# Other PSUM banks for the transposed blocks and the inverse transform's blocks in two stretches of a hand-ordered FFT and mixture-of-experts kernel

## The chip, the cores and the metric

The kernel runs on one core of a Trainium2 chip. The metric is the device time of one execution in microseconds (us). Three runs of the kernel before are known, and one profiled execution.

## What is computed

A filter in the frequency domain, then a layer of eight experts of which each token uses two:

```python
X = np.fft.rfft(x, axis=1)                       # x: 8 batches, 2496 tokens, 256 channels
y = np.fft.irfft(X * (filt_r + 1j * filt_i), n=2496, axis=1)
x = y.reshape(19968, 256)
noisy = x @ w_gate + np.log1p(np.exp(x @ w_noise)) * noise
top2 = np.argpartition(-noisy, 2, axis=1)[:, :2]     # two experts of eight
w = softmax over the two chosen values
for e in range(8):
    out[mask] += w * (np.maximum(x[mask] @ w1[e], 0) @ w2[e])   # 256 -> 1024 -> 256
```

## The kernel before

The transform of length 2496 is split as 39 x 64. One batch is two halves n of 128 channels each, so batch 0 is n = 0 and 1, batch 1 is n = 2 and 3. Each half goes through a chain of steps on TensorE, and each step writes one PSUM tile of 128 x 512 that ScalarE or VectorE copies out:

- `s1` (L320): the transform over 39, tile `q1` (in a few places `u3`); `kg1` (L401): the transform over 64, tile `q3`, then the product with the filter on VectorE (L424, L425); `kg2` (L434): the inverse over 64, tile `q4`, copied to `G` (L448).
- `logit_half` (L450), `logits` (L471), `gating` (L488): the gate's logits, tiles `u1`, `u2` and `lg`. From `lg` the generator `gate` (L744) works out the two experts of every token. This is a long row of small VectorE operations, with two exponentials and a logarithm on ScalarE (L757, L760, L790). Three times TensorE helps it with tiny matmuls: `rk` (L812 to L814) needs `rs` (L796); `sl` (L883, L884) needs `new` (L878); `st` (L908) needs `sval` (L904).
- `t3` (L506): four 128 x 120 blocks of `G` are transposed into tile `q5`, and ScalarE copies it to `tf` (L517). `i2` (L526): one matmul per `tf` into tile `q6`, the inverse over 39, which ScalarE copies to `yt` (L546) and a DMA writes to memory (L553). Each half has six such pairs.
- `route` (L918) turns the choice into a list of rows per expert, with tile `ra` (L950). Then the experts' blocks of up to 512 rows run: `turn` (L1061) makes the transposed rows, `expert` (L1149) multiplies with w1 in three passes (L123 to L125) into `hps` tiles, applies ReLU (L1181, L1182), and multiplies with w2 into `yps` tiles. Weights are split into two parts on ScalarE and VectorE (L1137, L1138).

TensorE runs the experts' first products between the last `t3` and `i2` of batch 1.

What sets the order. Batches 0 and 1 run "early", by a plan that is written out by hand: `plan` (L596 to L649) gives each of some 32 slots a list of steps. `pin` (L166) ties what each step issues on an engine behind what the step before it issued there. The gate's steps are traced at a place of the plan but are not tied; a scheduler places them when the program is built. For batch 1 the plan's slot 26 holds `logit_half`, `logits`, `gating`, then the first three `t3` and two `i2` and two `s1`; at that slot's end all of `rk`, `sl` and `st` are traced (L667 to L674). Slots 27 to 31 hold the other `t3`, `i2` and `s1`. Within an engine, the order is fixed once the program is built.

What sets the banks. PSUM has eight banks, given out under four tags. `ps` (L299) looks up the tag of a tile's name; names that are not in the table get `fps`. Tiles of one tag take its banks in turn, and a tile whose bank is still being read has to wait.

```python
EARLY = {"q1": "hps", "q2": "hps", "q5": "yps", "q6": "yps", "u1": "xps", "u3": "hps"}
BANKS = {"hps": 2, "yps": 2, "xps": 1, "fps": 3}
tag = self.banks.get(nm, "fps") if self.early else "fps"
return self.PS.tile([128, 512], F32, tag=tag, name=nm, bufs=BANKS[tag])
```

So `u2`, `lg`, `rk`, `sl`, `st` and `ra` always use the three `fps` banks. `MOVES` changes the table at the start of a slot: at slot 12, at slot 14 (where `t3` and `i2` of batch 0 share `hps`) and at slot 26 (where those of batch 1 share `yps`).

Of the kernel before, what the change touches and what calls it, by code (L numbers as in the profile page):

```python
# [137 lines left out]
EARLY = {"q1": "hps", "q2": "hps", "q5": "yps", "q6": "yps", "u1": "xps", "u3": "hps"}  # L138
BANKS = {"hps": 2, "yps": 2, "xps": 1, "fps": 3}

MOVES = {0: {"q3": "yps"}, 12: {"q3": "fps"}, 14: {"q3": "yps", "q4": "yps", "q5": "hps", "q6": "hps"}, 26: {"q1": "xps", "q4": "fps", "q5": "yps", "q6": "yps"}}


class Moe:
# [412 lines left out]
    def fft_stream(self):  # L557
# [105 lines left out]
        for t in range(max(plan) + 1):  # L663
            self.banks.update(MOVES.get(t, {}))
            for g in plan.get(t, []):
# [669 lines left out]
```

## Time and profile before

| what | value |
|---|---|
| median of three runs | 2246.81 us |
| lowest and highest run | 2244.74 and 2250.58 us |
| the profiled execution's own time | 2249.04 us |
| span of its profile | 2247.3 us |
| mean clock that TensorE was granted | 0.997 |
| TensorE matmuls busy | 2202.3 us (98%) |
| VectorE busy | 1614.5 us (72%) |
| ScalarE busy | 1227.9 us (55%) |
| GpSimd busy | 945.7 us (42%) |

A row of the timeline reads: start, duration, engine, line, operation, output<-input, shape, count, and in brackets the idle time before it with what ended it. Times in it are counted from the span's start. A row of the windows reads: the stretch, its length, then busy time of TensorE matmuls (PE), its weight loads (PEld), VectorE (DVE), ScalarE (ACT) and GpSimd (POOL) with counts, TensorE's granted clock, the DMA share and GB/s. A row of the waits reads: who waited for whom, the total in us, how often, and the longest.

### The profile page before, as it was taken

What the parts mean: (1) busy time and instruction counts of PE and PEld (TensorE: products, weight loads), DVE (VectorE), ACT (ScalarE), POOL (GpSimd) and SP (SyncE); (2) the same over time, 40 slices, a digit from 0 to 9 for tenths busy, and PEclk for the clock granted to TensorE, in tenths of its full rate; (3) what the DMA queues carried; (4) which work ended last, traced back from release to release, by engine and by line L of the source; (5) the groups of instructions that cost most, each with busy time, mean ns of one, the idle gap of its engine ahead of it and who ended that gap; (6) DMA issues with size and microseconds to landing.
All of it is one profiled execution on the core that took longest, in us unless ns stands there. A gap on an engine that the chain in (4) does not pass through costs nothing.

```text
span 2247.3 us, 39485 instructions
## 1 busy us (share of the span) xinstructions
PE 2202.3 (98%) x12687; PEld 1847.3 (82%) x12687; DVE 1614.5 (72%) x3482; ACT 1227.9 (55%) x2415; POOL 945.7 (42%) x824
## 2 busy tenths in 40 slices
PE   8999999999999999999999999999999999999998
PEld 6658888888888888888888888878888888888887
DVE  4777778779877968797668857796555556667776
ACT  6475655665565456545554445544444344557776
POOL 4014335334433543444434534444545454544442
PEclk9999999999999999999999999999999999999999
DMA  8768778987887677666665657556555557787774
GB/s 246 229 198 221 190 174 182 211 212 166 196 195 180 150 167 170 142 158 155 145 153 125 147 116 174 111 124 122 110 125 114 126 109 156 154 209 201 208 197 127
DMA packets 435434, 370.57 MB, mean 165 GB/s; under 512 B 185643, under 2 KB 345363, under 8 KB 435219
## 3 DMA queue, kind: packets, MB, share of 16 engines
q1 hardware_dynamic: 373907, 283.58, 46.7%
q0 software_dynamic: 61312, 84.40, 23.4%
q8 instruction: 101, 1.65, 0.3%
q14 instruction: 114, 0.93, 0.1%
HBM read 227.73 MB, written 105.25 MB: 148 GB/s over the span
## 4 chain that ended last, share of the span: by engine, by line
PE 89%; DVE 3%; DMA 3%; ACT 2%; issue 2%; SPq 0%; POOL 0%; another core or an unknown queue 0%; POOLq 0%; DVEq 0%; ACTq 0%
PE yps L1210 20%; PE hps L123 13%; PE hps L125 13%; PE hps L124 12%; PE yps L1211 10%; PE q L446 3%; PE yps L125 3%; PE yps L123 3%; PE yps L124 3%; PE q L512 1%; DMA stage<-w 1%; PE u L459 1%; PE q L536 1%; PE q L329 1%; PE q L534 1%
## 5 line engine op out<-in xcount | busy, mean ns | idle before, releaser
L1218 POOL DMA_INDIRECT out<-stage,ids x316 | 535.7, 1695 | 415.8 <-DVE stage L1217 224.4
L1210 PE MATMUL yps<-w,hh 128*128 128x512 f32 x1952 | 690.2, 398 | 4.0 <-DVE stage L1217 2.6
L1027 POOL DMA_INDIRECT stage<-y,ids x316 | 328.5, 1040 | 582.8 <-DMA xt<-stage 424.6
L124 PE MATMUL hps<-mxl,w1h 128*128 128x512 f32 (+2 forms) x1424 | 529.7, 374 | 1.5 <-DVE mxl L1091 1.5
L123 PE MATMUL hps<-mxh,w1h 128*128 128x512 f32 (+2 forms) x1424 | 518.9, 377 | 5.2 <-DVE hl L1182 3.7
L125 PE MATMUL hps<-mxh,w1l 128*128 128x512 f32 (+2 forms) x1424 | 523.9, 370 | 0.0
L1211 PE MATMUL yps<-w,hl 128*128 128x256 f32 x1952 | 521.7, 281 | 0.0
L1182 DVE SCALAR_TENSOR_TENSOR hl<-hps,hh 128x512 fp32r<-128x512 f32 (+2 forms) x712 | 433.5, 624 | 97.4 <-ACT hh L1181 88.1
L1181 ACT ACTIVATE hh<-hps 128x512 fp32r<-128x512 f32 (+2 forms) x712 | 381.5, 555 | 183.4 <-PE hps L125 163.6
L1210 PEld LDWEIGHTS yps<-w,hh 128*128 128x128 f32 x1952 | 356.7, 188 | 82.2 <-issue 5.3
L1211 PEld LDWEIGHTS yps<-w,hl 128*128 128x128 f32 x1952 | 367.1, 188 | 26.3 <-issue 0.6
L1215 ACT ACTIVATE stage<-yps,gt 128x256 f32<-128x256 f32 x316 | 142.3, 478 | 348.9 <-PE yps L1211 177.8
L125 PEld LDWEIGHTS hps<-mxh,w1l 128*128 128x128 f32 x1424 | 268.0, 188 | 48.1
L123 PEld LDWEIGHTS hps<-mxh,w1h 128*128 128x128 f32 x1424 | 263.4, 188 | 50.5 <-DVE hl L1182 9.1
L124 PEld LDWEIGHTS hps<-mxl,w1h 128*128 128x128 f32 x1424 | 268.1, 188 | 42.8 <-DVE mxl L1091 2.0
L1217 DVE SCALAR_TENSOR_TENSOR stage<-yps,gt,stage 128x256 f32<-128x256 f32 x244 | 112.1, 479 | 215.7 <-ACT stage L1215 185.3
L1137 ACT CAST w1h<-stage 128x512 fp32r<-128x512 f32 x192 | 119.2, 622 | 113.2 <-DMA stage<-w 52.9
L1138 DVE TENSOR_TENSOR w1l<-stage,w1h 128x512 fp32r<-128x512 f32 x192 | 130.8, 686 | 56.7 <-ACT w1h L1137 46.6
L123 PE MATMUL yps<-w,hh 128*128 128x256 f32 x576 | 163.4, 288 | 4.0 <-ACT hh L1181 3.0
L125 PE MATMUL yps<-w,hl 128*128 128x256 f32 x576 | 159.2, 285 | 1.1 <-DVE hl L1182 1.1
L124 PE MATMUL yps<-w,hh 128*128 128x256 f32 x576 | 160.1, 284 | 0.0
L1138 DVE TENSOR_TENSOR w<-stage,w 128x512 fp32r<-128x512 f32 x228 | 152.7, 685 | 6.7 <-ACT w L1137 5.3
(231 smaller groups left out, 3044.4 us busy)
## 6 DMA issues: line engine op xcount, KB each, us to landing
stage<-w SPq DMA_DIRECT2D x420, 256.0 KB
x<-x SPq DMA_DIRECT2D x88, 256.0 KB
wb<-w SPq DMA_DIRECT2D x18, 1024.0 KB
fx<-fd SPq DMA_DIRECT2D x140, 128.0 KB
fd<-c SPq DMA_DIRECT2D x73, 240.0 KB
out<-z SPq DMA_DIRECT2D x24, 702.0 KB
y<-yt SPq DMA_DIRECT2D x40, 248.6 KB
y<-yt SPq DMA_DIRECT2D x40, 234.0 KB
```

The lines of the kernel that those rows point to most:

```text
L123: nc.tensor.matmul(o, lh, rh, start=start, stop=False)
L124: nc.tensor.matmul(o, lh, rl, start=False, stop=False)
L125: return nc.tensor.matmul(o, ll, rh, start=False, stop=stop)
L1027: self.pin(lambda: nc.gpsimd.indirect_dma_start(out=x.bitcast(I32), out_offset=None, in_=self.y[:BLK + ready * ROWS], in_offset=bass.Indir ...
L1137: nc.scalar.copy(h, sv)
L1138: nc.vector.tensor_sub(l, sv, f32v(h))
L1181: r = nc.scalar.activation(h, p, AF.Relu)
L1182: v = nc.vector.scalar_tensor_tensor(l, p, 0.0, f32v(h), op0=ALU.max, op1=ALU.subtract)
L1210: nc.tensor.matmul(bank, h, hl, start=(f == 0), stop=False)
L1211: self.mm = nc.tensor.matmul(p, l, hl[:, 0], start=False, stop=(f == 7))
L1215: nc.scalar.activation(o, p, AF.Copy, scale=gate[:, t])
L1218: a = nc.gpsimd.indirect_dma_start(out=self.io["out"][:BLK + ready * ROWS], out_offset=bass.IndirectOffsetOnAxis(ap=ids[:, t:t + 1], axis= ...
```

## The change

One line of the table differs. From slot 14 on, `q5` (the `t3` tiles) goes to the one `xps` bank in place of the two `hps` banks, where `q6` (the `i2` tiles) stays. From slot 26 on, `q5` goes to the three `fps` banks in place of the two `yps` banks, where `q6` stays.

```diff
-MOVES = {0: {"q3": "yps"}, 12: {"q3": "fps"}, 14: {"q3": "yps", "q4": "yps", "q5": "hps", "q6": "hps"}, 26: {"q1": "xps", "q4": "fps", "q5": "yps", "q6": "yps"}}
+MOVES = {0: {"q3": "yps"}, 12: {"q3": "fps"}, 14: {"q3": "yps", "q4": "yps", "q5": "xps", "q6": "hps"}, 26: {"q1": "xps", "q4": "fps", "q5": "fps", "q6": "yps"}}
```

No instruction of the plan is added or taken away, but the built order moves. In the order, a tile's name carries its number; 1235 to 1415 are tiles of batch 1's gate (`u2`, `lg`, `rk`, `sl`, `st`), and `q5_1294` to `q5_1519` are `t3` tiles of batch 1.

First place: TensorE in slot 26, from the last `logit_half` on. Before, two `t3` stand ahead of the logits' transposes, and a third `t3` ahead of `lg`:

```order
L512 MATMUL q5_1294<-ident_70,G_974 120x128 x4
L512 MATMUL q5_1301<-ident_70,G_974 120x128 x4
L481 MATMUL u2_1221<-ident_70,ut0_1145 120x128 x3
L481 MATMUL u2_1227<-ident_70,ut1_1152 120x128
L481 MATMUL u2_1227<-ident_70,ut1_1152 120x96 x2
L534 MATMUL q6_1308<-tf_1299,cm_84 117x512
L512 MATMUL q5_1313<-ident_70,G_974 120x128 x4
L493 MATMUL lg_1235<-uh_1219,hl_76 117x352
```

Now, in the changed kernel, at the same place of TensorE:

```order
L481 MATMUL u2_1221<-ident_70,ut0_1145 120x128 x3
L481 MATMUL u2_1227<-ident_70,ut1_1152 120x128
L481 MATMUL u2_1227<-ident_70,ut1_1152 120x96 x2
L493 MATMUL lg_1235<-uh_1219,hl_76 117x352
L512 MATMUL q5_1294<-ident_70,G_974 120x128 x4
L494 MATMUL lg_1235<-ul_1220,hl_76 117x352
L495 MATMUL lg_1235<-uh_1219,hl_76 117x352
L512 MATMUL q5_1301<-ident_70,G_974 120x128 x4
```

The `t3` tiles, now under the gate's tag, come behind the gate's `u2` and `lg` tiles, which the plan traces ahead of them.

Second place: TensorE from the end of slot 26 into slot 27. Before, slot 27's first `t3` (`q5_1420`) follows the last `s1` of slot 26 at once:

```order
L534 MATMUL q6_1320<-tf_1306,cm_84 117x512
L329 MATMUL q1_1326<-x_1101,cm_84 120x512
L329 MATMUL u3_1331<-x_1103,cm_84 120x512
L512 MATMUL q5_1420<-ident_70,G_974 120x128 x4
L534 MATMUL q6_1427<-tf_1318,cm_84 117x512
L512 MATMUL q5_1432<-ident_70,G_974 120x128 x4
```

In the changed kernel the gate's six small matmuls stand between them:

```order
L534 MATMUL q6_1320<-tf_1306,cm_84 117x512
L329 MATMUL q1_1326<-x_1101,cm_84 120x512
L329 MATMUL u3_1331<-x_1103,cm_84 120x512
L812 MATMUL rk_1336<-rs_1280,small_77 117x8
L813 MATMUL rk_1336<-rs_1280,small_77 128x8
L814 MATMUL rk_1336<-small_77,rs_1280 8x1
L883 MATMUL sl_1394<-new_1387,small_77 8x1
L884 MATMUL sl_1394<-new_1387,small_77 8x1
L908 MATMUL st_1415<-sval_1404,small_77 1x64
L512 MATMUL q5_1420<-ident_70,G_974 120x128 x4
L534 MATMUL q6_1427<-tf_1318,cm_84 117x512
```

Before, the same `rk` stood 14 rows further on, and `sl` and `st` further still, among the experts' matmuls; this is where `sl` stood:

```order
L512 MATMUL q5_1519<-ident_70,G_1128 120x128 x4
L534 MATMUL q6_1526<-tf_1502,cm_84 117x512
L883 MATMUL sl_1394<-new_1387,small_77 8x1
L884 MATMUL sl_1394<-new_1387,small_77 8x1
L123 MATMUL hps_1887<-mxh0_1764,w1h_1741 128x512
```

All three groups of the gate's matmuls have moved ahead of `q5_1420`, and of everything that TensorE does behind it.

Third place: VectorE between `new` (L878), which `sl` needs, and the first operation on `sl` (L885). Before, work of the experts stands in between (`hl` of L1182, a weight part of L1138):

```order
L878 CAST new<-ci 8x1
L1182 SCALAR_TENSOR_TENSOR hl<-hps,hh 128x512
L838 TENSOR_REDUCE df<-rank_94 117x22
L855 TENSOR_SCALAR rf<-ri 56x1
L839 CAST di<-df 117x44
L1182 SCALAR_TENSOR_TENSOR hl<-hps,hh 128x512
L840 TENSOR_SCALAR di<-di 117x44
L1138 TENSOR_TENSOR w_1854<-stage,w_1854 128x512
L841 CAST hi<-di 117x44
L885 TENSOR_TENSOR st<-nblk,sl 8x1
```

Now only the gate's and the list's own operations stand there:

```order
L878 CAST new<-ci 8x1
L838 TENSOR_REDUCE df<-rank_94 117x22
L855 TENSOR_SCALAR rf<-ri 56x1
L885 TENSOR_TENSOR st<-nblk,sl 8x1
L839 CAST di<-df 117x44
L886 TENSOR_TENSOR nblk<-nblk,sl 8x1
L889 TENSOR_SCALAR en<-st 8x1
```

On ScalarE the exponential L790 moves likewise, from behind the copies of slot 28 to ahead of the copy of `q5_1420`. Through `sval` (L904) VectorE has none of the experts' work left among the gate's rows.

## The prediction

> **What bounds the kernel now.** I read the page's head and its chain that ended last, then TensorE's busy time by windows, its waits in the early stage, and the timelines of TensorE and VectorE there.
>
> ```profile
> PE 2202.3 (98%) x12687; PEld 1847.3 (82%) x12687; DVE 1614.5 (72%) x3482; ACT 1227.9 (55%) x2415; POOL 945.7 (42%) x824
> PE 89%; DVE 3%; DMA 3%; ACT 2%; issue 2%; SPq 0%; POOL 0%; another core or an unknown queue 0%; POOLq 0%; DVEq 0%; ACTq 0%
> ```
>
> TensorE is busy for 98% and carries 89% of the chain. So a microsecond in which it stands idle is lost, unless a later idle microsecond goes in exchange. Where is there any idle to exchange? The windows behind the place of the change:
>
> ```profile
> 122.00:144.00 22.00, 17.77 (x66) 9.41 (x65) 16.52 (x66) 19.51 (x33) 7.30 (x9) 0.92 0.81 238
> 144.00:160.00 16.00, 16.00 (x78) 10.57 (x76) 12.09 (x52) 12.99 (x24) 0.19 (x1) 1.00 0.60 180
> 160.00:180.00 20.00, 20.00 (x160) 18.29 (x159) 15.45 (x44) 12.10 (x25) 6.37 (x4) 1.00 0.79 213
> 180.00:200.00 20.00, 18.80 (x105) 16.04 (x104) 15.95 (x28) 10.77 (x20) 6.24 (x7) 1.00 0.80 208
> 200.00:240.00 40.00, 36.80 (x240) 31.11 (x239) 28.08 (x44) 24.72 (x47) 20.57 (x22) 1.00 0.92 223
> 240.00:280.00 40.00, 40.00 (x246) 35.31 (x245) 33.04 (x53) 25.75 (x46) 12.09 (x11) 1.00 0.78 186
> 280.00:320.00 40.00, 37.78 (x256) 33.15 (x255) 27.40 (x59) 22.62 (x46) 15.69 (x13) 1.00 0.72 161
> ```
>
> Idle TensorE: 22.00 - 17.77 = 4.2 us in 122 to 144, none from 144 to 180, then 1.2 + 3.2 + 0 + 2.2 = 6.6 us up to 320. These are all that the change can win or get back nearby. TensorE's waits between 20 and 170 us that touch the changed tiles and the gate:
>
> ```profile
> PE q L534 <- ACT yt L546: 3.2, 6, 0.9
> PE q L512 <- ACT tf L517: 2.4, 2, 2.2
> PE rk L812 <- DVE rs L796: 1.7, 1, 1.7
> ```
>
> The first two are a matmul that waits until ScalarE has emptied its bank: 5.6 us in both batches together. That is the whole prize.
>
> **The first batch (slots 14 to 17).** `t3` and `i2` alternate in two banks, so each already has one of its own; now `t3` has the single `xps` bank and `i2` two. The waits for `yt` in these slots (62 to 92 us) and ahead of them (50 to 62 us, where the old banks stay):
>
> ```profile
> PE q L534 <- ACT yt L546: 0.9, 2, 0.7
> PE q L534 <- ACT yt L546: 0.8, 2, 0.7
> ```
>
> So 0.9 us is at stake. But behind it comes the `rk` of batch 0, which waited 1.7 us for VectorE, and a TensorE that arrives earlier only waits longer there. I take -0.3 us, between 0 and -0.9.
>
> **The second batch (slot 26 on).** TensorE's timeline, the gate's matmuls among it:
>
> ```profile
> 118.63 0.32 PE L495 MATMUL lg<-uh,hl 120*117 120x352 f32 x1
> ...
> 120.81 1.02 PE L329 MATMUL u<-x,cm 117*120 117x512 f32 x2
> 121.66 0.60 PE L512 MATMUL q<-ident,G 128*120 128x128 f32 x4
> ...
> 125.59 0.65 PE L512 MATMUL q<-ident,G 128*120 128x128 f32 x4 [2.21 <-ACT tf L517]
> 126.50 2.05 PE L534 MATMUL q<-tf,cm 120*117 120x512 f32 x2 [0.26 <-issue]
> ...
> 136.27 0.28 PE L812 MATMUL rk<-rs,small 117*117 117x8 f32 x2
> ...
> 146.97 0.19 PE L883 MATMUL sl<-new,small 8*8 8x1 f32 x2
> ...
> 157.01 0.27 PE L908 MATMUL st<-sval,small 8*1 8x64 f32 x2
> ```
>
> Before, TensorE goes from `s1` to slot 27's first `t3` at 121.66, and meets `rk`, `sl` and `st` at 136, 147 and 157 us, when VectorE has long had what they need. In the new order all six stand ahead of that `t3`. TensorE works in order, so it now stands still until VectorE has run the gate from `lg` to `sval`; behind it wait all `t3`, `i2`, `s1` and the first expert's matmuls, and with them ScalarE's copies. When does `st` run? VectorE's rows:
>
> ```profile
> 127.05 0.69 DVE L1138 TENSOR_TENSOR w1l<-stage,w1h 128x512 fp32r<-128x512 f32 x1 [1.02 <-ACT w1h L1137]
> 127.66 0.33 DVE L770 TENSOR_TENSOR gz<-gl,lg 117x176 f32<-117x176 f32 x1
> 127.91 0.68 DVE L1138 TENSOR_TENSOR w1l<-stage,w1h 128x512 fp32r<-128x512 f32 x1
> 128.51 0.33 DVE L780 TENSOR_REDUCE m<-gz 117x22 f32<-117x176 f32 x1
> ...
> 131.28 0.12 DVE L438 MEMSET G<- 128x80 f32 x1 [1.69 <-PE q L512]
> ...
> 135.01 0.46 DVE L796 TENSOR_REDUCE rs<-rank 117x8 f32<-117x176 f32 x1
> ```
>
> - *To `rk`.* L770 starts at 127.66. In the new order it stands behind two weight parts (L1138) instead of three, but ScalarE's casts for them come behind two `i2` copies that are later; I keep 127.7, give or take 2. From L770 to the end of `rs` are 135.47 - 127.66 = 7.8 us. The weight part at 127.91 (0.6) and the MEMSET's wait (1.7) are no longer in between, and six operations on the gate's weights (L803 to L809) are: the rows below start 0.1 and 0.25 us ahead of their next, three of each kind, about 1.1. So 7.8 - 0.6 - 1.7 + 1.1 = 6.6, and `rk` runs at 134.3.
>
> ```profile
> 137.27 0.18 DVE L803 TENSOR_SCALAR gs<-ge 117x22 f32<-117x22 f32 x1 [1.79 <-ACT ge L790]
> 137.37 0.33 DVE L800 TENSOR_TENSOR rank<-rank 117x176 f32<-117x176 f32 x1
> 138.10 0.33 DVE L807 TENSOR_TENSOR dense<-oh,gs 117x176 f32<-117x176 f32 x1
> 138.35 0.33 DVE L800 TENSOR_TENSOR rank<-rank 117x176 f32<-117x176 f32 x1
> ```
>
> - *To `sl`.* Batch 0 shows this piece without foreign work in it:
>
> ```profile
> 77.08 0.37 PE L812 MATMUL rk<-rs,small 117*117 117x8 f32 x2 [1.69 <-DVE rs L796]
> 77.83 0.16 DVE L822 SCALAR_TENSOR_TENSOR rw<-mm,rk 128x8 int32<-128x8 f32 x1
> 81.51 0.13 DVE L878 CAST new<-ci 8x1 f32<-8x1 int32 x1
> ```
>
> From `rk` to L822 are 0.75 us, from L822 to the end of L878 81.64 - 77.83 = 3.8. So `sl` runs at 134.3 + 4.6 = 138.9.
>
> - *To `st`.* From L885 to the end of L904:
>
> ```profile
> 147.25 0.14 DVE L885 TENSOR_TENSOR st<-nblk,sl 8x1 f32<-8x1 f32 x1 [0.22 <-PE sl L884]
> 149.84 0.69 DVE L1182 SCALAR_TENSOR_TENSOR hl<-hps,hh 128x512 fp32r<-128x512 f32 x1
> 151.66 0.69 DVE L1138 TENSOR_TENSOR w1l<-stage,w1h 128x512 fp32r<-128x512 f32 x1 [0.89 <-ACT w1h L1137]
> ...
> 153.00 0.67 DVE L1138 TENSOR_TENSOR w<-stage,w 128x512 fp32r<-128x512 f32 x1
> 154.05 0.22 DVE L904 TENSOR_SCALAR sval<-sge,small 8x32 f32<-8x32 f32 x1
> ```
>
> 7.0 us, of which four operations of the experts (first and last shown, 0.6 each) and a wait of 0.9 go: 3.7. Three small casts come in and one list operation moves out, so 4.0. With 0.3 from `sl` to L885, `st` runs at 138.9 + 0.3 + 4.0 = 143.2, and the `t3` starts at 143.5 in place of 121.66: **21.8 us later**. Bounds: L770 may be 2 us earlier or later.
>
> What comes back of this: 0.9 us, since `rk`, `sl` and `st` no longer cost later (0.4, 0.2 and 0.3). Of the 4.2 us of idle in 122 to 144, the waits for a shared bank go, but ScalarE was busy for 19.51 of those 22 us, so after the stall its copies pace `t3` and `i2`; I let 2.7 come back, between 0 and 4.2. From 144 to 180 nothing can come back. Of the 6.6 us up to 320 I let 1.5 come back, between 0 and 6.6, for weights, gathers and the gate's VectorE work are then ahead.
>
> The clock: after its wait of 2.2 us the matmul pair at 126.50 took 2.05 us where the one at 120.81 took 1.02, and the window's granted clock is 0.92. The restart after the new stall costs the same, so I count 0, and up to +1.7.
>
> The Trainium skill, TensorE: Matmul & The Clock Gate, part 1, says that an idle window of about 3.4 us halves the clock and that it returns after about as long a busy one. By that rule the restart would lose an estimated 1.7 us; the trace agrees that the clock falls, with its 0.92, though a wait of only 2.2 us preceded it.
>
> Sum: -0.3 + 21.8 - 0.9 - 2.7 - 1.5 = **+16.4 us**. On the profiled execution's 2249.0 this makes 2265.4; that execution lies 2.2 us above the median of the runs, 2246.8, on which it makes **2263 us**.
>
> **The rivals.**
>
> *All is given back.* L770 comes 2 us earlier, all idle up to 320 (4.2 + 6.6) and batch 0's 0.9 go: 21.8 - 2 - 0.9 - 10.8 - 0.9 = +7.2, or 2254, and 2253 with one more us of idle behind 320, which is no difference. Against it: 144 to 180 is full, and the idle behind is spread over many short waits of the experts. 6%.
>
> *More is lost.* ScalarE, already at 19.51 of 22, gives nothing back (+2.7), L770 is 2 us later, the clock costs 1.7, nothing returns behind 180 (+1.5): +24.3, or 2271. For it: ScalarE's casts stand ahead of L770. 13%.
>
> *Faster.* This rests on one mechanism: `st` is ready when TensorE reaches it, so the moved matmuls cost nothing and the emptied banks count. Price: the waits of 5.6 less the 0.8 ahead of slot 14, and some 1.8 lost to the low clock after the wait of 2.2: -6.6, or 2240. It decides whether the gate, from `lg` to `sval`, lasts under the 3 us between the row at 118.63 and 121.66; batch 0 alone needs 3.8 from `rk` to `new`. 3%.
>
> The Trainium skill, Perfetto Trace Analysis, section Matmuls, says that independent groups of matmuls should rotate through different PSUM banks, so that emptying one overlaps the next group. By that rule the change gains; the trace agrees as far as the 5.6 us of waits for full banks go, and it says nothing of a tag whose banks also hold the gate's tiles.
>
> **How the numbers follow.** The forecast has 78%. Within 0.3% (6.7 us, about what a measurement of this kernel can tell from no change) ends at 2253.5. The range runs from the first rival's 2253 to just above the second's 2271, so to 2272. Slower 78 + 13 = 91%, same 6%, faster 3%.
>
> **What would show it.** In the profile after: `rk` waits some 8 us for `rs`, `sl` about 4 for `new`, `st` about 4 for `sval`, all between 126 and 144; slot 27's first `t3` starts near 143.5; the first expert's L1181, at 143.6 before, comes 15 to 19 us later. Waits of L534 for `yt` and L512 for `tf` fall well below 5.6. The prediction is wrong if that `t3` starts ahead of 135, or if the idle behind 180 falls by more than 6.

## The result, and the profile after

| | before | after |
|---|---|---|
| median | 2248.69 us (2244.74 to 2253.05, 4 runs) | 2268.15 us (2266.14 to 2272.94, 4 runs) |
| the profiled execution | 2249.04 us, span 2247.3 | 2266.14 us, span 2264.3 |
| mean granted clock of TensorE | 0.997 | 0.992 |

The ratio is 1.0084 (95% interval 1.0065 to 1.0102), or about +18.9 us: slower. Forecast were +16.4 us and 2263 us, between 2253 and 2272. Between the two profiled executions, on which the sum was made, the difference is +17.0 us of span. One execution of one kernel further down (`t3` in the single bank) took 3592.70 us at a granted clock of 0.556; it is in no median or ratio here.

The page of the kernel after, engines:

```profile
PE 2203.0 (97%) x12687; PEld 1849.4 (82%) x12687; DVE 1614.6 (71%) x3482; ACT 1229.1 (54%) x2415; POOL 954.1 (42%) x824
```

TensorE does the same work (2202.3 before). Its idle time grew from 2247.3 - 2202.3 = 45.0 to 2264.3 - 2203.0 = 61.3 us, so 16.3 of the 17.0 us are idle time. Where it lies, by the windows of the kernel after (TensorE's busy time is the second number):

```profile
122.00:144.00 22.00, 4.79 (x23) 3.16 (x23) 18.36 (x94) 4.96 (x9) 2.78 (x5) 0.61 0.24 70
144.00:160.00 16.00, 15.57 (x63) 8.82 (x61) 4.07 (x7) 15.75 (x28) 3.83 (x4) 1.00 0.67 199
160.00:180.00 20.00, 18.32 (x91) 12.32 (x89) 9.07 (x24) 13.93 (x26) 0.19 (x1) 1.00 0.62 173
180.00:200.00 20.00, 20.00 (x151) 17.89 (x150) 15.97 (x42) 12.61 (x25) 8.12 (x5) 1.00 0.78 212
200.00:240.00 40.00, 36.70 (x222) 32.31 (x221) 29.98 (x47) 22.25 (x40) 19.47 (x21) 0.96 0.88 217
240.00:280.00 40.00, 40.00 (x255) 34.13 (x254) 31.29 (x50) 27.68 (x52) 13.27 (x14) 1.00 0.81 202
280.00:320.00 40.00, 38.27 (x252) 33.01 (x251) 28.51 (x50) 24.32 (x49) 12.59 (x11) 1.00 0.75 194
```

In 122 to 144 us 17.2 us are idle, 4.2 before: +13.0. In 144 to 180 us it is 2.1 against none, and up to 320 us 3.3 + 1.7 = 5.0 against 6.6. TensorE's waits in 20 to 190 us (total, how often, longest) name the three that the prediction named:

```profile
PE rk L812 <- DVE rs L796: 12.4, 2, 9.4
PE sl L883 <- DVE new L878: 4.1, 1, 4.1
PE st L908 <- DVE sval L904: 3.7, 1, 3.7
PE q L512 <- ACT tf L517: 1.5, 2, 1.3
PE q L534 <- ACT yt L546: 0.8, 2, 0.7
```

The row of `rk` holds both batches: 9.4 us in batch 1, 3.0 in batch 0. The last two rows are the waits for a shared bank, the prize; `t3` and `i2` now lose less there. In the timeline of TensorE the last `logit_half` (L459), the last matmul of `lg` (L495) and the stall read:

```profile
112.56 1.41 PE L459 MATMUL u<-G,wg 128*32 128x360 f32 x16 [0.68 <-ACT G L448]
...
117.28 0.33 PE L495 MATMUL lg<-uh,hl 120*117 120x352 f32 x1
...
121.07 1.02 PE L329 MATMUL u<-x,cm 117*120 117x512 f32 x2
131.46 0.53 PE L812 MATMUL rk<-rs,small 117*117 117x8 f32 x2 [9.37 <-DVE rs L796]
136.66 0.18 PE L883 MATMUL sl<-new,small 8*8 8x1 f32 x2 [4.12 <-DVE new L878]
140.63 0.37 PE L908 MATMUL st<-sval,small 8*1 8x64 f32 x2 [3.73 <-DVE sval L904]
140.93 1.11 PE L512 MATMUL q<-ident,G 128*120 128x128 f32 x4
141.83 1.91 PE L534 MATMUL q<-tf,cm 120*117 120x512 f32 x2
```

The last `s1` of slot 26 starts at 121.07 us (120.81 before). Then three matmuls that take about a microsecond together, and 9.37 + 4.12 + 3.73 = 17.2 us of waiting; slot 27's first `t3` starts at 140.93 us, not at 121.66. And VectorE, from the gate's L770 to `sval`:

```profile
124.95 0.33 DVE L770 TENSOR_TENSOR gz<-gl,lg 117x176 f32<-117x176 f32 x1
130.85 0.46 DVE L796 TENSOR_REDUCE rs<-rank 117x8 f32<-117x176 f32 x1
132.59 0.16 DVE L822 SCALAR_TENSOR_TENSOR rw<-mm,rk 128x8 int32<-128x8 f32 x1
136.38 0.13 DVE L878 CAST new<-ci 8x1 f32<-8x1 int32 x1
136.93 0.14 DVE L885 TENSOR_TENSOR st<-nblk,sl 8x1 f32<-8x1 f32 x1
140.35 0.22 DVE L904 TENSOR_SCALAR sval<-sge,small 8x32 f32<-8x32 f32 x1
```

VectorE is busy for 18.36 of the 22 us from 122 to 144: from L770 to `sval` its rows follow one another with hardly a gap, and TensorE waits for them. Not all of them are the gate's: of the 3.6 us between L885 and the end of `sval`, 2.3 are rows of the list of tokens (L839 to L842, L945 to L947) that stand among the gate's. While TensorE stands, ScalarE and the transfers come to a stand too. ScalarE's next copy and SP's own queue:

```profile
142.12 0.59 ACT L517 COPY tf<-q 120x512 f32<-120x512 f32 x1 [13.51 <-PE q L512]
```

```profile
SPq L985 <- DVE tabi L916: 16.5, 1, 16.5
```

SP reads a register from the table `tabi` (L985), which VectorE makes from `st` (L916). It stood at that read for 16.5 us, up to 141.5, and every DMA that it issues stood behind it. The next one in its order, a store of `yt`, then waited on for ScalarE's copy and was issued at 144.8 us; so the read was not the only thing that held the queue. The transfers did not run ahead in the stall. The windows within it show it in the last two columns (DMA share and GB/s; before, these three read 296, 207 and 100 GB/s):

```profile
128.00:132.00 4.00, 0.54 (x3) 0.57 (x4) 3.92 (x17) 0.22 (x1) 0.18 (x1) 0.50 0.04 16
132.00:136.00 4.00, 0.55 (x4) 0.43 (x4) 3.65 (x29) 0.00 (x0) 0.00 (x0) 0.50 0.01 2
136.00:140.00 4.00, 0.23 (x4) 0.17 (x4) 3.89 (x30) 0.00 (x0) 0.00 (x0) 0.50 0.00 0
```

### The profile page after: what moved, and what is told of

Its sections match the earlier page's. It is cut to its first block, busy times and chain, and to the rows that moved or that the text cites. A ratio compares the mean times of both kernels' runs of the same rounds, so it can differ in the third digit from the quotient of the medians.

```text
span 2264.3 us, 39492 instructions
## 1 busy us (share of the span) xinstructions
PE 2203.0 (97%) x12687; PEld 1849.4 (82%) x12687; DVE 1614.6 (71%) x3482; ACT 1229.1 (54%) x2415; POOL 954.1 (42%) x824
## 4 chain that ended last, share of the span: by engine, by line
PE 89%; DVE 4%; ACT 3%; issue 2%; DMA 2%; SPq 0%; POOL 0%; another core or an unknown queue 0%; ACTq 0%; DVEq 0%; POOLq 0%
PE yps L1210 19%; PE hps L123 13%; PE hps L125 12%; PE hps L124 12%; PE yps L1211 10%; PE q L446 3%; PE yps L123 3%; PE yps L125 3%; PE yps L124 2%; PE q L512 1%; PE u L459 1%; DMA stage<-w 1%; DVE hl L1182 1%; PE q L536 1%; PE q L537 1%
## 5 line engine op out<-in xcount | busy, mean ns | idle before, releaser
L1218 POOL DMA_INDIRECT out<-stage,ids x316 | 541.3, 1713 | 420.9 <-DVE stage L1217 219.2
L1182 DVE SCALAR_TENSOR_TENSOR hl<-hps,hh 128x512 fp32r<-128x512 f32 (+2 forms) x712 | 432.8, 623 | 97.3 <-ACT hh L1181 82.6
L1181 ACT ACTIVATE hh<-hps 128x512 fp32r<-128x512 f32 (+2 forms) x712 | 380.9, 554 | 186.8 <-PE hps L125 169.5
L1138 DVE TENSOR_TENSOR w1l<-stage,w1h 128x512 fp32r<-128x512 f32 x192 | 130.8, 685 | 54.5 <-ACT w1h L1137 46.2
L1138 DVE TENSOR_TENSOR w<-stage,w 128x512 fp32r<-128x512 f32 x228 | 152.4, 684 | 6.6 <-ACT w L1137 5.8
```

Source lines behind the costliest of these rows:

```text
L1138: nc.vector.tensor_sub(l, sv, f32v(h))
L1181: r = nc.scalar.activation(h, p, AF.Relu)
L1182: v = nc.vector.scalar_tensor_tensor(l, p, 0.0, f32v(h), op0=ALU.max, op1=ALU.subtract)
L1218: a = nc.gpsimd.indirect_dma_start(out=self.io["out"][:BLK + ready * ROWS], out_offset=bass.IndirectOffsetOnAxis(ap=ids[:, t:t + 1], axis= ...
```

## The experiments

The theory: the time is lost because `rk`, `sl` and `st` now stand ahead of slot 27's `t3` in TensorE's order, and TensorE waits there for the whole gate. The rivals: the new banks cost by themselves; the first part of the change costs; the later order or the cold clock costs more than the waits. Each kernel is compared with the kernel before, run beside it on the same chip; its median lay at 2234.7 and 2234.9 us for the first eight kernels and at 2249.2 us for the last two. The only profile of the kernel before is that of the result. TensorE's busy time in it is 2202.3 us, and 2192 to 2200 us in the profiles of the first eight, so a difference of a microsecond or two between their windows and its own need not come from the edit.

### The first part alone, and the second part alone

Slot 14 as after and slot 26 as before, and the other way round:

```diff
-26: {"q1": "xps", "q4": "fps", "q5": "fps", "q6": "yps"}
+26: {"q1": "xps", "q4": "fps", "q5": "yps", "q6": "yps"}
```

```diff
-14: {"q3": "yps", "q4": "yps", "q5": "xps", "q6": "hps"}
+14: {"q3": "yps", "q4": "yps", "q5": "hps", "q6": "hps"}
```

> Only the first batch's part of the change: from slot 14 on the t3 tiles take the xps bank; slot 26 is as before. Theory (the stall): the loss is TensorE standing still for rk, sl and st behind slot 26, which this kernel does not have, so it is no slower than before: -1.3 us, as TensorE reached batch 1's logits 1.3 us earlier in the profile after; 2245 to 2250. Rival (the banks of the first batch, or the altered order behind it, carry part of the loss): 3 us or more slower than before.

> Only the second batch's part: from slot 26 on the t3 tiles take the fps banks; slot 14 is as before. Theory (the stall): waits of rk, sl and st of 9.4 + 4.1 + 3.7 = 17 us stay, and the first batch's 1.3 us are not won: 18 to 22 us slower than before. Rival (the two parts are lossy only together, or the first part carries the loss): under 10 us slower.

Measured: the first part alone 2233.31 us, ratio 0.9984 (0.9973 to 0.9996), about -3.6 us. The second part alone 2254.44 us, ratio 1.0087 (1.0074 to 1.0101), about +19.4 us, with the same three waits as the whole change (9.4, 4.1 and 3.7 us) and its `t3` at 142.14 us. So the second part carries all of the loss, and the rival of the first part falls. The kernel with the first part alone is the only one here that is faster than the kernel before, by a little.

In the kernel with the first part alone, TensorE's waits in 20 to 190 us hold batch 0's `rk`:

```profile
PE rk L812 <- DVE rs L796: 3.0, 1, 3.0
```

It rose from 1.7 to 3.0 us, as the prediction said of a TensorE that arrives earlier. The gain came all the same, and not in batch 0: from 50 to 100 us TensorE idles 6.0 us, 4.8 before. In 280 to 320 us it idles 0.3 us, 2.2 before, but the two kernels below that lack the first part and keep the old banks idle 0 there, so this cannot be laid on the first part. Where the gain comes from is not shown.

### The order alone

Banks as before; the gate's matmuls of batch 1 are tied into TensorE's order at the place where they are traced, as the plan's other steps are:

```diff
-                self.pin(self.gating_more, gating[0], hold=False)
+                k = dict(hold=True, only=[self.nc.tensor.engine]) if t >= 26 else dict(hold=False)
+                self.pin(self.gating_more, gating[0], **k)
```

> All banks as before; only the order on TensorE is forced: batch 1's rk, sl and st are tied into the written order on TensorE, so that they stand ahead of slot 27's first t3. Theory (the stall): the order alone costs the loss: rk, sl and st wait about 17 us together, and the kernel is 13 to 20 us slower than before. Rival (the banks themselves, three shared banks for t3 and what else they carry, cost the time): within 4 us of before.

Measured: 2251.62 us, ratio 1.0076 (1.0062 to 1.0090), about +17.0 us. The timeline of TensorE (this kernel's lines are numbered one higher):

```profile
131.36 0.56 PE L813 MATMUL rk<-rs,small 117*117 117x8 f32 x2 [10.79 <-DVE rs L797]
136.50 0.19 PE L884 MATMUL sl<-new,small 8*8 8x1 f32 x2 [4.02 <-DVE new L879]
140.56 0.37 PE L909 MATMUL st<-sval,small 8*1 8x64 f32 x2 [3.82 <-DVE sval L905]
140.86 1.11 PE L512 MATMUL q<-ident,G 128*120 128x128 f32 x4
```

No bank differs from the kernel before, and the stall and the loss are there. (The list's `ra` comes earlier in this kernel as well, at 143.5 us, behind the stall.) The order suffices. Together with the kernel below that keeps the new banks without this order, this settles the cause.

### Only rk ahead

As the changed kernel, but `sl` and `st` take the single `xps` bank and `q1` goes to `hps`, so that of the gate only `rk` stands ahead of the `t3`:

```diff
-26: {"q1": "xps", "q4": "fps", "q5": "fps", "q6": "yps"}
+26: {"q1": "hps", "q4": "fps", "q5": "fps", "q6": "yps", "sl": "xps", "st": "xps"}
```

> As the changed kernel, but from slot 26 on sl and st take the xps bank (and the s1 tiles that had it take hps), so that of the gate's matmuls only rk stands ahead of slot 27's first t3; sl follows three t3 later and st two more. Theory (the stall): rk keeps its wait of 9 us, sl and st find their input ready, so the loss falls from 18.9 by 4.1 + 3.7 = 7.8 to 9 to 13 us. Rival (the loss is the restart of a cold clock and the altered later order, not the length of the waits): 17 us or more slower, as the changed kernel.

Measured: 2248.98 us, ratio 1.0057 (1.0043 to 1.0071), about +12.7 us. The timeline of TensorE:

```profile
132.76 0.53 PE L812 MATMUL rk<-rs,small 117*117 117x8 f32 x2 [8.87 <-DVE rs L796]
133.78 1.11 PE L512 MATMUL q<-ident,G 128*120 128x128 f32 x4
...
158.98 2.06 PE L534 MATMUL q<-tf,cm 120*117 120x512 f32 x2 [3.82 <-ACT tf L517]
```

`sl` and `st` have no wait left, and the loss is smaller by some 6 us of the 7.9 that they had. A new wait of 3.8 us for a copy of ScalarE, late in the chain, may be why the loss is more than `rk`'s own wait; the clock is low behind it (0.79 in 160 to 180 us). No run tries it alone.

### t3 not behind the gate, in two ways

One kernel gives the gate the `xps` bank and leaves `t3` in `fps` and `i2` in `yps`, as in the changed kernel; the other gives `t3` the `xps` bank and leaves the gate in `fps`:

```diff
-26: {"q1": "xps", "q4": "fps", "q5": "fps", "q6": "yps"}
+26: {"q1": "hps", "q4": "fps", "q5": "fps", "q6": "yps", "rk": "xps", "sl": "xps", "st": "xps"}
```

```diff
-26: {"q1": "xps", "q4": "fps", "q5": "fps", "q6": "yps"}
+26: {"q1": "hps", "q4": "fps", "q5": "xps", "q6": "yps"}
```

> From slot 26 on the gate's tiles rk, sl and st take the single xps bank for themselves, and t3 keeps the fps banks with i2 in yps, as in the changed kernel; slot 14's part stays. So TensorE's order has rk behind five of slot 27's t3 and no t3 stands behind a gate tile. My theory (the time is lost because TensorE stands in order behind the gate's matmuls): no wait of rk, sl or st above 1 us, slot 27's first t3 near 121 us again, and the time from 7 us below the kernel before to level with it (ratio 0.997 to 1.000). Rival (t3 in the fps banks, or i2 alone in yps, costs by itself, through ScalarE's copies or VectorE's use of these banks): +8 us or more although no gate matmul waits.

> From slot 26 on t3 takes the single xps bank and the piece that had it (q1) goes to hps; i2 stays in yps, and the gate's tiles are alone in the fps banks. t3 has one bank where the changed kernel gives it two, but it is not behind the gate. My theory: no wait of rk, sl or st above 1 us, and between 5 us below and 4 us above the kernel before, since a single bank makes t3 wait for its copy (L512 on tf, up to 3 us in all). Rival (what matters is how many banks t3 has, and the order only follows): clearly slower than the changed kernel's +18.9 us, since one bank is fewer than two.

Measured: with the gate in its own bank 2235.35 us, ratio 1.0007 (0.9998 to 1.0016). TensorE's timeline there:

```profile
133.62 0.28 PE L812 MATMUL rk<-rs,small 117*117 117x8 f32 x2
144.12 0.19 PE L883 MATMUL sl<-new,small 8*8 8x1 f32 x2
149.45 0.27 PE L908 MATMUL st<-sval,small 8*1 8x64 f32 x2
```

No wait, and no loss that can be told from none, with `t3` and `i2` in the very banks of the changed kernel. The rival that these banks cost 8 us or more falls. But there is no gain either, although the first part is in it: against 0.9984 for the first part alone, this second part looks some 5 us worse than the old banks. Some of that may be due to `q1`, which had to give up `xps` for `hps` in this kernel, in the next one and in the one with only `rk` ahead; that move was not tried alone. Its windows:

```profile
122.00:144.00 22.00, 19.08 (x67) 9.54 (x65) 19.04 (x82) 20.34 (x34) 7.34 (x9) 0.92 0.78 221
144.00:160.00 16.00, 13.63 (x89) 8.76 (x88) 11.11 (x53) 9.33 (x19) 0.18 (x1) 1.00 0.81 243
```

In the first window TensorE idles 2.9 us, 4.2 before, and each wait left is for a copy of ScalarE, which is busy for 20.34 of 22 us: whatever the bank, it has little to spare. The 1.3 us won there are lost again in the second window, with 2.4 us of idle against none, in short waits for ScalarE and VectorE. There ScalarE is busy for only 9.33 of 16 us, so a full ScalarE does not explain them.

With `t3` in the single bank: 2239.90 us, ratio 1.0023 (1.0014 to 1.0032), about +5.1 us, one microsecond above what was expected. In batch 1 no wait of the gate is above 0.5 us, but `t3` waits 7.6 us for its copies in 20 to 190 us. One bank for `t3` is far better than three behind the gate; the rival that counts banks falls.

### The gate's matmuls traced later

The banks are those of the changed kernel, but the gate's part is emitted two slots later, and in another kernel five:

```diff
-            if gating:
+            if gating and not 26 <= t < 28:
```

> All banks as in the changed kernel; the gate's part of batch 1 (from the ranks to the list of tokens) is emitted two slots later, so that four of slot 27's t3 and their i2 stand ahead of rk, and some of the experts' matmuls between rk, sl and st. My theory: the stall shrinks by the TensorE work that now stands ahead and in between. rk waits 0 to 5 us, sl 0 to 4, st 0 to 4; in all 3 to 9 us of waits in place of 17.2, and the time is 2 to 10 us above the kernel before (ratio 1.001 to 1.0045). Rival (the length of the gate chain, not its place in TensorE's order, sets the loss): within 4 us of the changed kernel's +18.9 us.

> All banks as in the changed kernel; the gate's part of batch 1 is emitted five slots later, so that all but the last of slot 27's t3 stand ahead of rk. My theory: no wait of rk, sl or st above 1.5 us; what is left is the gain of the separate banks, against a later list of tokens, so between 6 us below and 4 us above the kernel before (ratio 0.997 to 1.002). Rival (the banks of the changed kernel cost by themselves): +8 us or more without such waits. Second rival (the later list holds up batch 1's gathers and with them its experts): new waits of TensorE for gathered tokens behind 560 us, 5 us or more.

Measured: two slots later 2243.51 us, ratio 1.0047 (1.0033 to 1.0061); five slots later 2244.37 us, ratio 1.0045 (1.0032 to 1.0058). In both, no wait for `rs`, `new` or `sval` is left in batch 1, so half of the loss is gone. The other half, about 10 us, is not, and for this the theory had expected less: at most 10 and at most 4. It lies elsewhere. Two slots later, in 122 to 180 us:

```profile
122.00:144.00 22.00, 16.64 (x68) 10.50 (x67) 18.13 (x72) 17.36 (x29) 5.45 (x7) 0.92 0.78 232
144.00:160.00 16.00, 12.32 (x49) 7.24 (x48) 10.66 (x41) 11.00 (x18) 0.72 (x1) 1.00 0.28 78
160.00:180.00 20.00, 17.12 (x128) 13.13 (x127) 9.44 (x34) 10.75 (x21) 1.65 (x1) 1.00 0.81 229
```

TensorE idles 11.9 us there, against 5.4 in the kernel with the gate in its own bank, in many waits for ScalarE and VectorE. The longest, 3.2 us, is that of `turn` (L1087) for ScalarE's copy of an `s1` tile (L378); the experts' matmuls wait 2.9 us for VectorE (L1182, L1091). Five slots later it idles at 200 to 240 us:

```profile
180.00:200.00 20.00, 20.00 (x163) 18.48 (x161) 12.62 (x44) 6.93 (x13) 4.67 (x3) 1.00 0.17 28
200.00:240.00 40.00, 32.00 (x146) 24.00 (x146) 28.97 (x46) 21.31 (x39) 15.60 (x18) 0.79 0.83 215
```

8.0 us idle, against 3.0. Just ahead, the DMA share is 0.17, and SP's queue had stood 13.6 us for `xl` of VectorE (L334) and 9.7 us at L985. VectorE runs this `xl` right behind the list's row L954, at 195.4 us, and at 175.1 us in the kernel before. Here the later gate, with the later list, holds up the transfers. The second rival had looked for this elsewhere: behind 560 us no wait for gathered tokens appears. The rival that the changed kernel's banks cost by themselves, 8 us or more, would give these two times as well; the kernel with the gate in its own bank speaks against it for `t3` and `i2`. What share of the 10 us is due to which wait is open.

### A longer gate, in the new order and in the old

22 small VectorE operations more in batch 1's gate alone, which multiply by one: 12 on `new` behind L878 and 10 on `sval` ahead of `st`, once in the changed kernel and once in the kernel before:

```diff
-        v.tensor_copy(new, ci)
+        v.tensor_copy(new, ci), [v.tensor_scalar_mul(new, new, 1.0) for _ in range(12 * (len(self.tabs) == 1))]
```

> The changed kernel with 22 more small VectorE operations in batch 1's gate alone: 12 that multiply new by one between the cast that makes it and sl (about 0.2 us each when one waits for the other, 2.4 us), and 10 that multiply half of sval by one ahead of st (about 0.25 us each, 2.5 us). TensorE's order is that of the changed kernel. My theory (TensorE has nothing else to do while the gate runs, so the gate's length is paid one for one): sl waits 6 to 7 us in place of 4.1, st 5.5 to 6.5 in place of 3.7, and the time is 3.5 to 6 us above the changed kernel's, ratio to the kernel before 1.0100 to 1.0111. Rival (a longer stall is mostly taken up by the idle time behind it, as ScalarE and the transfers get ahead): the waits grow, but the ratio stays within 1.0075 to 1.0093.

> The kernel before with the same 22 VectorE operations in batch 1's gate. sl and st are not held at a place there, and they come behind more of the experts' matmuls. My theory (in the old order other matmuls cover the gate): no wait of rk, sl or st above 1 us, and 0 to 4 us above the kernel before, the upper end for the later list of tokens (ratio 1.000 to 1.0018). Rival (the gate's length is paid in the old order as well): 4.5 us or more (1.0020 or more).

Measured: in the changed kernel 2272.85 us, ratio 1.0101 (1.0084 to 1.0118), 0.0017 or 3.8 us above the changed kernel's 1.0084. TensorE's waits in 20 to 190 us:

```profile
PE rk L812 <- DVE rs L796: 12.4, 2, 9.4
PE sl L883 <- DVE new L878: 8.3, 1, 8.3
PE st L908 <- DVE sval L904: 3.9, 1, 3.9
```

The waits are 4.3 us longer in sum, nearly all of it at `sl` (8.3 us, where 6 to 7 were expected) and hardly any at `st` (3.9, where 5.5 to 6.5 were). From `sl` to `sval` VectorE took 1.8 us in place of 3.7, since the list's rows now stand among the added ones ahead of `sl`. The time grew by about as much. The ratio's interval reaches down into the rival's, so that the gate's length is paid in full is what the waits say, and the time only agrees.

In the kernel before: 2254.17 us, ratio 1.0021 (1.0011 to 1.0030), about +4.7 us (2.5 to 6.7), where the theory had expected at most 4 and the rival at least 4.5; the interval does not decide between them. No wait for the gate appears; the program's order has `sl` and `st` further behind instead. But some of the gate's length is paid in the old order too, in another place: SP's queue

```profile
SPq L315 <- DVE xl L334: 12.9, 1, 12.9
```

stands in 165 to 205 us (before, the longest there is 4.3), the DMA share in 180 to 200 us is 0.34 (0.80 before), and TensorE idles 7.2 us in 200 to 240 us (3.2 before). The `xl` that SP waits for starts at 186.3 us, again behind the list's row L954. So the old order kept TensorE from waiting for the gate, but a longer gate still delays the list and what stands behind it.

## Why the prediction was right, point by point

- **What bounds it.** TensorE's busy time did not move (2202.3 and 2203.0 us); 16.3 of the 17.0 us are idle time. Right.
- **The first batch, -0.3 us (0 to -0.9).** Mis-sized: the first part alone brought -3.6 us (-0.9 to -6.0). The wait of `rk` grew as said, by 1.3 us. What failed is the bound, which counted only the waits within the slots. Where the 3.6 us come from is not shown. In the changed kernel nothing of it is seen at the stall: the last `s1` ahead of it starts 0.26 us later than before.
- **L770 at 127.7.** It started at 124.95, 2.7 us earlier, just outside the 2 us allowed. Half of it lies far ahead of the stall: the last `logit_half` (L459) already starts 1.34 us earlier (112.56, not 113.90), and `lg` with it. Nothing shows that this is an effect of the first part: L459 starts anywhere between 111.0 and 114.4 us in the kernels here, latest with the first part alone. The other half is VectorE's: from the last matmul of `lg` to L770 it took 7.7 us in place of 9.0, without the wait of 1.02 us for a weight part.
- **From L770 to st.** To `rk` 131.46 - 124.95 = 6.5 us (6.6 was worked out), to `sl` 5.2 (4.6), to `st` 4.0 (4.3), and 0.3 to the `t3`. So 16.0 us against 15.8: the piece-wise sum held, and the `t3` came 19.3 us later, not 21.8, by the start of L770.
- **The waits.** 9.4, 4.1 and 3.7 us where 8, 4 and 4 were to show it, all between 122 and 141 us.
- **What comes back at once, 0.9 + 2.7 us.** The lag is 19.3 us at that `t3` and 160.04 - 146.01 = 14.0 us at the seventh `i2` from there (`q6_1526`), so 5.2 us came back. The `rk`, `sl` and `st` that no longer stand later are in it, and the waits for `yt` and `tf`. The first expert's L1181 came at 157.40 us, 13.8 us later; 15 to 19 had been said; had L770 not come 2.7 us earlier than said, 13.8 would have been 16.5. This `i2`, before and then after:

```profile
146.01 1.02 PE L534 MATMUL q<-tf,cm 120*117 120x512 f32 x2
```

```profile
160.04 1.02 PE L534 MATMUL q<-tf,cm 120*117 120x512 f32 x2
```

- **The idle time up to 320 us, -1.5 us.** It fell from 6.6 to 5.0 us: right. From 320 to 560 us it fell by another 1.7, but in 560 to 900 us it grew by 2.1 us, with one wait of 1.9 us of L536 for ScalarE's copy of `G` (0.2 before); no step had that. And the stretch from 144 to 180 us, full before, now idles 2.1 us.
- **The reason given for it,** that transfers would then be ahead, was wrong: SP's queue stood with TensorE, and 0 to 16 GB/s moved in 128 to 140 us.
- **The clock, 0.** The granted clock was 0.50 in 128 to 140 us, and the first pair behind the stall took 1.11 and 1.91 us where 0.60 and 1.02 are usual, 1.4 us more; the three matmuls of `rk` took 0.5 us more than before. Before, the pair at 126.50 had lost 1.0 us in the same way, and the `s1` behind it (first row below) 0.7. So the restart came to about what it had cost before, and 0 was right. The Trainium skill (TensorE: Matmul & The Clock Gate, part 1) has the clock return after about 3.4 us of work; the trace roughly agrees, with a granted clock of 0.50 up to 143.7 us and of 1.00 from 143.8 on, 3.1 us after `st` at 140.63.

```profile
128.35 1.76 PE L329 MATMUL q<-x,cm 117*120 117x512 f32 x2
129.95 1.02 PE L329 MATMUL u<-x,cm 117*120 117x512 f32 x2
```

- **The rivals.** *Faster* asked that the gate be ready within 3 us; from `lg` (117.28) to the end of `sval` (140.57) it took 23. *All is given back* asked for 10.8 us of idle time in exchange; by 560 us 5.4 came back (the 4.2 of 122 to 144, less the 2.1 that are new up to 180, and 3.3 behind). *More is lost* was the nearer one: the median lies 5 us above the forecast and 3 below this rival's 2271. Of these 5 us, 1.9 are the base: with a fourth run the median of the kernel before is 2248.69 and not 2246.81.

The sum thus came out near the profiled difference (+16.4 and +17.0 us) with errors that offset each other; that it came this near is luck, the mechanism is not. The `t3` was put 2.5 us too late, and 1.6 us too little was let come back behind it: -4.1. Against this, from `q6_1526` (14.0 us late) to the end (17.0) another 3.0 us were lost, where 1.5 were to come back: +4.5. Half of the 3.0 is work that the new order only put behind `q6_1526`: up to there TensorE idled 15.5 us more, by the windows from 50 to 160 us, but was 14.0 us late.

The Trainium skill (Perfetto Trace Analysis, section Matmuls) advises that independent groups of matmuls rotate through different PSUM banks. The first part followed it and won 0.16%. The second followed it too and, alone, lost 0.87%, since the new banks belonged to a tag that also held tiles of a slow chain; with that chain in another bank, and both parts in, the ratio was 1.0007. So these runs agree with the advice for the first part by a little, and for the second not at all: with the gate out of the way of `t3`, nothing was gained that can be told from none.

## What to carry to other kernels

Before moving a tile to another pool or tag, list what else takes that tag's banks and in what order it is traced: in these kernels the built order of TensorE followed that order within a tag, and TensorE stood behind the slowest of the tiles. Price such a move by the chain that it puts in front, piece by piece from the trace, and ask which queues (here SP's) stand with it, since they can't run ahead and pay the loss back. Waits for a full bank are worth little where the engine that empties it has little to spare, here ScalarE with 20.34 of 22 us.

## What the runs showed of the hardware

- The granted clock fell to 0.50 within the stall and the first matmuls behind it took 1.11 and 1.91 us, nearly twice the usual 0.60 and 1.02; a matmul pair of the kernel before had already lost half its speed (2.05 us) after a wait of only 2.2 us. In windows of 0.1 us the clock is low from 126.4 to 129.8 us before, which is 3.4 us, and from 126.7 to 143.7 us after, which is 17.1 or five times 3.4. Before, it fell 0.8 us after TensorE had gone back to work, at 125.6 us.
- SP's queue stood for 16.5 us at one read of a register from a table (L985) that VectorE had not yet written, and then for a copy of ScalarE; it issued no DMA from 125.0 to 144.8 us. In 128 to 140 us 0 to 16 GB/s were moved, where 100 to 296 had been moved before.
- Of the VectorE operations that were added, the ten on `sval` took 2.01 us, 0.2 each; those on `new` came up to 1.3 us apart, with other steps in between, so that the twelve held `sl` up by 4.2 us where 2.4 had been worked out.
